# Attention loop of a fused attention and feed-forward kernel: whole loads, row-tiled scores, an earlier decay table, and projections put behind the loop

## The chip, the cores and the metric

The program runs on one core of a Trainium2 chip. Times are microseconds (us) of device time for one launch. Three runs before the change gave a median of 637.87 us (lowest 637.09); the third, 2779.6 us, was a disturbed run and is not used below. Five engines run their own instruction streams in order: PE (matrix products into the 8 banks of PSUM), ACT (activations), DVE (vector), POOL (GpSimd) and SP, which here only starts transfers.

## The reference

Three blocks follow each other. The first is causal linear attention with decay over 2 batches, 8 heads, 768 positions and 64 features, in blocks of 64:

```python
intra = np.einsum('bhic,bhjc->bhij', qb, kb) * Dmask[None]
intra = np.einsum('bhij,bhjd->bhid', intra, vb)
inter = np.einsum('bhid,bhde->bhie', qb * lam_pow[None], kv_state)
out[:, :, sl] = intra + inter
kv_state = lam_block[None, :, None, None] * kv_state + np.einsum('bhsd,bhse->bhde', kb_dec, vb)
```

`Dmask` holds powers of a head's `lam` below the diagonal. The result, 1536 tokens of 512 features, goes through `g(x @ w_in) @ w_out` (2048 hidden features, `g` a clipped square) and then through `(sigmoid(x @ w_gate) * (x @ w_val)) @ w_out` (1536 hidden features).

## The kernel before

**Attention.** The work is cut into 16 units (batch, pair of heads, half of the sequence), each with three chunks of 128 positions. Units 0 to 7 are batch 0. A unit has four products on PE: scores (L412), state updates (L427), and the outputs, from weighted scores (L475) and from states (L484). DVE multiplies the scores by the decay table `DT` (`pT`, L442) and runs the states forward (`sc`, L453), ACT copies states into block-diagonal tiles (`st`, L465), and the output leaves as two float parts, `xh` by ACT (L494) and `xl` by DVE (L495). POOL makes the decayed keys `kd` (L388) and the decayed queries `qs` (L398). `kd` and `pT` need `DT`, `qs` and `sc` need `qp`. Loop i (`for i in range(nu)`) issues scores, updates and `pT` of unit i + 1, `kd` of unit i + 2, outputs of unit i, and `qs` of unit i + 2.

**Tables.** For heads 0 and 1 DVE builds `DT` in 14 steps (L349) and ACT builds `qp` (L354, L357). For the other heads ACT builds rows of powers in `pw` (L360, L363), which go out to DRAM (`pd`, L365) and come back spread over the partitions as `qp` (L370) and `DT` (L375). All these transfers are on SP's queue, among the loads of the units.

**Feed-forward.** A product of float32 accuracy is made of three products of high and low parts. A step of the first block for a slice n of 128 hidden features and a third t of the tokens is `hidden` (12 products, L147 to L149), its activation (L173 to L175), the split into `gh` and `gl` (L165, L166) and `project` (12 products, L202); there are 48 such steps, and 36 of the second block with 24 and 12 products, 2448 products in all. `steps` is a generator that gives such steps one by one. While `rounds` is empty, that is in the attention loop, each `next(steps)` gives either one `hidden` or one `project`. t = 0 needs units 0 to 7 only; t = 1 needs unit 14. Before, the calls stand in loops 7 to 12, 14 and 15.

**Weights.** They come as 68 pieces of 128 x 512 doubles and are turned into two float32 parts in rounds (`w_round`), one piece per stage: ACT takes both words (L85, L86), DVE shifts and joins (L92, L93), `eng` adds (L95), ACT rounds to the high part (L99), `eng` subtracts for the low part (L103). In the attention loop rounds stand in loops 1, 3 and 5 to 12 with POOL as `eng`; behind it DVE does them.

**Order.** `manual_schedule` keeps the written order for each engine, but for a few instructions at the seam between the two blocks of it. Loads and tables wait in SP's stream in order. `wp` is a ring of 14 slots for weight pieces; in its first two lie `q_diag`, copies of the queries of units 0 and 1 with zeros beside each head, so that their scores use 128 rows.

Of the kernel before, what the change touches and what calls it, by code (L numbers as in the profile page):

```python
# [7 lines left out]
F32 = mybir.dt.float32  # L8
# [19 lines left out]
CST = 4 + PADW + P  # L28
FFREE = (13,)
NQD = 2  # L30
NWP, NRAW = 14, 5


@with_exitstack
def fused_kernel(ctx: ExitStack, tc: tile.TileContext, qkv, qd, cst, w1, w2, out):
# [70 lines left out]

    def w_round(eng=dve, between=None):
        k = prog["round"]
        if k - 2 >= len(pieces):
            return  # L110
        if k - 2 >= NWP and pieces[k - 2 - NWP][0] >= prog["done"]:
            return
        prog["round"] += 1
        if 0 <= k - 1 < len(pieces):
            w_float(k - 1, eng)
        if between:
            between()
# [113 lines left out]
    def feed_forward(rounds):  # L231
# [17 lines left out]
        for u in seq:  # L249
# [26 lines left out]
    with ExitStack() as actx:  # L276
# [17 lines left out]
        def u_part(i, o, n):  # L294
            b, p, h = units[i]
            sp.dma_start(out=raw_u[i][:, o:o + n], in_=qkv[b, p, h][:, o:o + n])

        q_diag = {}  # L300

# [3 lines left out]
        DT = kp.tile([P, H, P], F32, name="DT")  # L305
        qp = kp.tile([P, NP, P], F32, name="qp")
        pw = tp.tile([P, 512], F32, tag="c", name="pw")[0:H, 0:2 * P]
        pd = dp.tile([H, 2 * P], F32, name="pd")
# [3 lines left out]
        st = [kp.tile([P, 2 * CU - 1, P], F32, name=f"st{j}") for j in range(2)]  # L312

        def tables():

            cs = tp.tile([P, 512], F32, tag="r", bufs=3, name="cs")
            dm = [tp.tile([P, 512], F32, tag="r", bufs=3, name=f"dm{j}")[:, 0:2 * (PADW + P)]
                  .rearrange("p (h x) -> p h x", h=2) for j in range(2)]
            sp.dma_start(out=cs[:, 0:CST], in_=cst)
            for i in range(NQD):  # L320
                u_load(i)
                q_diag[i] = wp.tile([P, 2, 512], F32, tag="w", name=f"qd{i}").rearrange(
                    "p a b -> p (a b)")[:, 0:2 * UT].rearrange("p (c e t) -> p c e t", c=CU, e=2)
                u_part(i, 1, 1)
                for c in range(CU):
                    if c < 2 or i:
                        c1 = CU if c or i else 1
                        sp.dma_start(out=q_diag[i][:, c:c1], in_=qd[i][:, c:c1])
                    if i:
                        break  # L330
            for i in range(NQD):
                u_part(i, 2, 2)
            for i in range(NQD):
                u_part(i, 0, 1)
            for j in range(2):
# [5 lines left out]
            act.activation(st[1], st[0], AF.Copy)  # L341
            sq = [cs[:, 0:2]] + [cs[:, CST + 2 * k:CST + 2 * k + 2] for k in range(6)]
            for k in range(7):
                w = 1 << k
                if k:
                    pool.tensor_tensor(out=sq[k], in0=sq[k - 1], in1=sq[k - 1], op=ALU.mult)
                for h in range(2):
                    src = cs[:, 4:CST] if k == 0 else dm[k % 2][:, h]
# [4 lines left out]
                    )  # L353
            act.activation(qp[:, 0, 0:1], cs[:, 3:4], AF.Copy)  # L354
            for k in range(7):
                w = 1 << k
                act.activation(qp[:, 0, w:2 * w], qp[:, 0, 0:w], AF.Copy,  # L357
                               scale=qp[:, 0, w - 1:w])

            act.activation(pw[:, P:P + 1], cs[0:H, 2:3], AF.Copy)  # L360
            for k in range(7):
                w = 1 << k
                act.activation(pw[:, P + w:P + 2 * w], pw[:, P:P + w], AF.Copy,  # L363
                               scale=pw[:, P + w - 1:P + w])
            sp.dma_start(out=pd, in_=pw)  # L365
            u_load(2)
            w_load()
            pdv = pd[:, :]
            for e in range(2):
# [4 lines left out]
                )  # L374
            sp.dma_start(  # L375
                out=DT[:, 2:],
                in_=bass.AP(pdv.tensor, pdv.offset + 4 * P, [[1, P], [2 * P, H - 2], [1, P]]),
            )
            u_load(3)
            w_load()  # L380

        S_ps, U_ps, pT, qs, kd, xs = {}, {}, {}, {}, {}, {}

        def pre_k(i):
# [3 lines left out]
            pool.tensor_tensor(  # L388
                out=kd[i], in0=raw_u[i][:, 2].rearrange("p (c h d) -> p c h d", c=CU, h=2),
                in1=DT[:, 2 * p:2 * p + 2, P - 1:P].unsqueeze(1).to_broadcast([P, CU, 2, D]),  # L390
# [3 lines left out]
        def pre_q(i):  # L394
# [3 lines left out]
            pool.tensor_tensor(  # L398
                out=qs[i], in0=raw_u[i][:, 0].rearrange("p (c t) -> p c t", c=CU),
                in1=qp[:, p:p + 1, :].to_broadcast([P, CU, P]), op=ALU.mult,  # L400
            )

        def scores(i):
# [5 lines left out]
            for c in range(CU):  # L409
                for e in range(2):  # L410
                    r = slice(0, P) if i in q_diag else slice(e * D, (e + 1) * D)
                    pe.matmul(  # L412
                        S_ps[i][e][:, c * P:(c + 1) * P], lhsT=u[r, 1, c * P:(c + 1) * P],
                        rhs=q_diag[i][:, c, e] if i in q_diag else u[r, 0, c * P:(c + 1) * P],
                        start=True, stop=True,
                    )

        def updates(i):
# [3 lines left out]
            for c in range(CU):  # L422
                if h * CU + c == 2 * CU - 1:
                    continue
                for e in range(2):
                    r = slice(e * D, (e + 1) * D)
                    pe.matmul(  # L427
                        t[r, c * D:(c + 1) * D], lhsT=kd[i][:, c, e],
                        rhs=u[:, 3, c * P + e * D:c * P + (e + 1) * D],
                        start=True, stop=True,  # L430
# [36 lines left out]
        def outputs(i):  # L467
# [4 lines left out]
            for c in range(CU):  # L472
                for e in range(2):
                    r = slice(e * D, (e + 1) * D)
                    pe.matmul(  # L475
                        x[r, c * P:(c + 1) * P],
                        lhsT=u[:, 3, c * P + e * D:c * P + (e + 1) * D],
                        rhs=pT[i][:, e, c * P:(c + 1) * P],
# [20 lines left out]

        with tc.manual_schedule():  # L500
            tables()
            scores(0)
            scores(1)
# [8 lines left out]
            for i in range(nu):  # L512
# [92 lines left out]
```

## Time and profile before

| what | value |
|---|---|
| median of the runs shown | 637.87 us |
| the profiled execution's own time | 638.09 us |
| its span, first to last instruction | 636.3 us |
| mean granted clock of PE | 0.983 |
| PE busy | 614.8 us, 97% |
| DVE, ACT, POOL busy | 352.5, 287.2, 56.8 us |
| loads and stores | 53.37 MB |

PE is the busiest engine over the span, but the span has stages: up to 96.5 us attention products are mixed with feed-forward products, behind it PE runs feed-forward products without a gap. A busy share over the whole span says nothing of the first stage. The profiled execution took 1.8 us more than its span.

### The profile page before, as it was taken

How to read it: one execution, taken by the hardware profiler on the slowest of the kernel's cores; microseconds unless marked ns; L12 is line 12 of the kernel's file. 1: busy time of each engine (PE TensorE's matmuls, PEld its weight loads, DVE VectorE, ACT ScalarE, POOL GpSimd, SP SyncE). 2: the span in 40 equal slices, each digit the busy share in tenths (PEclk: the TensorE clock that was granted, in tenths of full speed). 3: DMA queues.
4: the chain of work that ended last, by engine and by line, in shares of the span. 5: the costliest groups of instructions: out<-in, count | busy, mean ns of one | idle time of the engine just before them, and what ended most of it. 6: DMA issues, size and time to landing. Idle time of an engine off the chain costs nothing.

```text
span 636.3 us, 7871 instructions
## 1 busy us (share of the span) xinstructions
PE 614.8 (97%) x3072; PEld 507.7 (80%) x3072; DVE 352.5 (55%) x612; ACT 287.2 (45%) x511; POOL 56.8 (9%) x62
## 2 busy tenths in 40 slices
PE   6779889999999999999999999999999999999997
PEld 5667668888888888888888888888888888888886
DVE  4485864655666666666776912157843167713132
ACT  5356745665565556556675612144721145311110
POOL 3486740000000000000000000000000000000000
PEclk9789979999999999999999999999999999999999
DMA  8985520322132223122213400024420022001011
GB/s 262 349 291 220 199 66 1 101 66 67 66 100 66 67 67 91 56 60 92 66 34 99 133 0 1 1 66 133 132 67 0 1 59 74 1 1 67 0 67 66
DMA packets 16229, 53.37 MB, mean 84 GB/s; under 512 B 1720, under 2 KB 3648, under 8 KB 16192
## 3 DMA queue, kind: packets, MB, share of 16 engines
q1 hardware_dynamic: 16192, 52.87, 25.5%
q8 instruction: 24, 0.39, 0.3%
q14 instruction: 13, 0.11, 0.0%
HBM read 49.71 MB, written 3.15 MB: 83 GB/s over the span
## 4 chain that ended last, share of the span: by engine, by line
PE 88%; ACT 4%; DVE 4%; DMA 2%; issue 1%; POOL 1%; SPq 0%; POOLq 0%; ACTq 0%; DVEq 0%
PE a L202 35%; PE h L147 17%; PE h L148 17%; PE h L149 17%; DVE pT L442 1%; DMA DT<-pd 1%; PE x L484 1%; PE x L475 1%; ACT xh L494 1%; ACT st L465 1%; PE s L412 1%; DVE sc L453 1%; DMA pd<-pw 1%; DVE r L175 0%; DVE part L216 0%
## 5 line engine op out<-in xcount | busy, mean ns | idle before, releaser
L147 PE MATMUL h<-xh,w 128*128 128x512 f32 x480 | 188.3, 392 | 0.0
L148 PE MATMUL h<-xh,w 128*128 128x512 f32 x480 | 187.7, 391 | 0.0
L149 PE MATMUL h<-xl,w 128*128 128x512 f32 x480 | 187.3, 390 | 0.0
L202 PE MATMUL a<-gh,w 128*128 128x512 f32 x384 | 118.7, 390 | 0.5 <-DVE r L175 0.5
L148 PEld LDWEIGHTS h<-xh,w 128*128 128x128 f32 x480 | 90.7, 189 | 19.0 <-POOL w L103 0.3
L149 PEld LDWEIGHTS h<-xl,w 128*128 128x128 f32 x480 | 90.6, 189 | 18.9
L147 PEld LDWEIGHTS h<-xh,w 128*128 128x128 f32 x480 | 90.7, 189 | 18.6
L181 DVE TENSOR_TENSOR r<-r,h 128x512 f32<-128x512 f32 x36 | 24.7, 687 | 139.4 <-PE h L149 137.1
L202 PE MATMUL a<-w,gh 128*128 128x512 f32 x288 | 88.6, 389 | 0.0
L202 PEld LDWEIGHTS a<-gh,w 128*128 128x128 f32 x384 | 71.8, 188 | 15.5 <-DVE r L175 0.9
L175 DVE SCALAR_TENSOR_TENSOR r<-r,h 128x512 f32<-128x512 f32 x48 | 33.0, 687 | 87.1 <-ACT r L174 87.0
L165 ACT ACTIVATE gh<-r 128x512 fp32r<-128x512 f32 x84 | 52.4, 624 | 60.8 <-DVE r L181 55.5
L202 PE MATMUL a<-gl,w 128*128 128x512 f32 x192 | 74.7, 389 | 0.0
L173 ACT ACTIVATE r<-h,half 128x512 f32<-128x512 f32 x48 | 33.0, 688 | 91.5 <-PE h L149 91.5
L166 DVE TENSOR_TENSOR gl<-r,gh 128x512 fp32r<-128x512 f32 x84 | 58.4, 695 | 16.5 <-ACT gh L165 16.4
L202 PEld LDWEIGHTS a<-w,gh 128*128 128x128 f32 x288 | 54.1, 188 | 11.2
L180 ACT ACTIVATE r<-h 128x512 f32<-128x512 f32 x36 | 21.5, 597 | 87.2 <-PE h L149 87.2
L99 ACT ACTIVATE w<-wr 128x512 fp32r<-128x512 f32 x68 | 42.4, 623 | 39.6 <-DVE wr L95 39.2
L202 PE MATMUL a<-w,gl 128*128 128x512 f32 x144 | 56.0, 389 | 0.0
L93 DVE SCALAR_TENSOR_TENSOR wr<-raw,wr 128x512 uint32<-128x512 uint32 x68 | 50.1, 737 | 2.3
L85 ACT ACTIVATE wr<-raw 128x512 f32<-128x512 f32 x68 | 45.1, 664 | 0.8 <-POOL w L103 0.8
L86 ACT ACTIVATE wc<-raw 128x512 int32<-128x512 uint32 x68 | 44.8, 658 | 0.0
(51 smaller groups left out, 513.5 us busy)
## 6 DMA issues: line engine op xcount, KB each, us to landing
raw<-in_w SPq DMA_DIRECT2D x68, 512.0 KB, 3.6
u<-in_qkv SPq DMA_DIRECT2D x14, 768.0 KB, 5.7
out<-part SPq DMA_DIRECT2D x12, 256.0 KB, 2.1
u<-in_qkv SPq DMA_DIRECT2D x4, 192.0 KB, 5.6
u<-in_qkv SPq DMA_DIRECT2D x2, 384.0 KB, 6.2
qd<-in_qd SPq DMA_DIRECT2D x1, 384.0 KB, 5.4
DT<-pd SPq DMA_DIRECT2D x1, 384.0 KB, 6.3
qd<-in_qd SPq DMA_DIRECT2D x1, 256.0 KB, 3.7
```

Source lines behind the costliest of these rows:

```text
L85: act.activation(r, hi.bitcast(F32), AF.Copy, scale=2.0 ** -112)
L86: act.activation(c, lo, AF.Copy, scale=2.0 ** -29)
L93: dve.scalar_tensor_tensor(out=ru, in0=hi, scalar=0x80000000, in1=ru, op0=ALU.bitwise_and, op1=ALU.bitwise_or)
L99: act.activation(ws[i][:, 0], tmps[i][1], AF.Copy)
L147: pe.matmul(h, lhsT=wh, rhs=xh[:, k, tt], start=(k == 0), stop=False)
L148: pe.matmul(h, lhsT=wl, rhs=xh[:, k, tt], start=False, stop=False)
L149: pe.matmul(h, lhsT=wh, rhs=xl[:, k, tt], start=False, stop=(k == NP - 1))
L165: act.activation(gh, g, AF.Copy)
L166: dve.tensor_tensor(out=gl, in0=g, in1=gh.bitcast(F32), op=ALU.subtract)
L173: act.activation(r, h, AF.Relu, bias=half, scale=0.5)
L175: dve.scalar_tensor_tensor(out=r, in0=r, scalar=1.0, in1=h, op0=ALU.min, op1=ALU.max)
L202: pe.matmul(accs[j], lhsT=a, rhs=b_, start=(f == 0 and m == 0), stop=(f == GF - 1 and m == 2))
```

## The change

It does these things:

- The first four units load into two slots each of `wp`, as halves (q and k, then k and v by rows), with whole slices; units 0 to 2 are loaded ahead of all tables. Loads of later units are asked for two loops earlier (`u_load(i + 6)`), into the same four buffers.
- `q_diag` and its input are no longer used: scores of units 0 and 1 use 64 rows like the others.
- `warm` gives PE two products of zeros ahead of the first scores.
- ACT's queue loads the constants and stores `pd`; ACT builds `pw` ahead of `qp`; `DT` comes back in two transfers, heads 2 and 3 first. DVE builds its two tables one head after the other.
- Rounds stand in loops 3 to 6 and 8 to 14. Up to loop 6 DVE subtracts for the low part, later POOL.
- `next(steps)` stands in loops 7, 9, 11 and 13, and gives one `hidden` each; no `project` is given in the loop. Behind it the generator first catches up with two of them.

```diff
-FFREE = (13,)
+HIDDEN = (7, 9, 11, 13)
+ROUNDS = (3, 4, 5, 6, 8, 9, 10, 11, 12, 13, 14)
 NQD = 2
+NEARLY = 4
+WARM = 2
...
-    def w_round(eng=dve, between=None):
+    def w_round(eng=dve, between=None, low=dve):
...
         if 0 <= k - 2:
-            w_low(k - 2, eng)
+            w_low(k - 2, low)
...
-            flushed = False
-            if len(behind) == LAG:
+            while len(behind) >= (LAG if rounds else LAG + 1):
                 flushed = finish()
-                if not rounds:
-                    yield u
-            if rounds:
                 if ph:
...
-            raw_u[i] = up.tile([P, 4, UT], F32, tag="u", name=f"u{i}")
-            if i >= NQD:
-                sp.dma_start(out=raw_u[i], in_=qkv[b, p, h])
...
+            if i < NEARLY:
+
+                t = [wp.tile([P, 2, 512], F32, tag="w", name=f"u{i}_{j}")
+                     .rearrange("p a b -> p (a b)")[:, 0:2 * UT]
+                     .rearrange("p (a t) -> p a t", a=2) for j in range(2)]
+                for j in range(2):
+                    sp.dma_start(out=t[j], in_=qkv[b, p, h][:, 2 * j:2 * j + 2])
+            else:
+                a = up.tile([P, 4, UT], F32, tag="u", name=f"u{i}")
+                sp.dma_start(out=a, in_=qkv[b, p, h])
...
+        def warm():
+
+            z = bank("z")
+            for _ in range(WARM):
+                pe.matmul(z, lhsT=zero[:, 0:P], rhs=zero, start=True, stop=True)
...
-            sp.dma_start(out=cs[:, 0:CST], in_=cst)
-            for i in range(NQD):
+            act.dma_start(out=cs[:, 0:CST], in_=cst)
+            for i in range(3):
                 u_load(i)
...
-            sp.dma_start(out=pd, in_=pw)
-            u_load(2)
-            w_load()
...
+            act.dma_start(out=pd, in_=pw)
...
-            sp.dma_start(
-                out=DT[:, 2:],
-                in_=bass.AP(pdv.tensor, pdv.offset + 4 * P, [[1, P], [2 * P, H - 2], [1, P]]),
-            )
+            for h0, h1 in ((2, 4), (4, H)):
+                sp.dma_start(
+                    out=DT[:, h0:h1],
+                    in_=bass.AP(pdv.tensor, pdv.offset + h0 * 2 * P,
+                                [[1, P], [2 * P, h1 - h0], [1, P]]),
+                )
             u_load(3)
+            u_load(4)
+            w_load()
+            u_load(5)
             w_load()
...
-                    r = slice(0, P) if i in q_diag else slice(e * D, (e + 1) * D)
+                    r = slice(e * D, (e + 1) * D)
...
             tables()
+            warm()
             scores(0)
...
-                if i in (1, 3) or 5 <= i <= 12:
-                    w_round(pool, finish)
+                if i in ROUNDS:
+                    w_round(pool, finish, pool if i >= nu // 2 else dve)
...
-                u_load(i + 4)
+                u_load(i + 6)
                 w_load()
-                if i >= nu // 2 - 1 and i not in FFREE:
+                if i in HIDDEN:
                     next(steps)
```

The first place is ACT's stream at the start. Before:

```order
L341 ACT_TABLE_LOAD
L341 ACTIVATE st_98<-st_97 128x640
L354 ACTIVATE qp<-cs 128x1
L357 ACTIVATE qp<-qp 128x1
...
L360 ACTIVATE pw<-cs 8x1
L363 ACTIVATE pw<-pw 8x1
...
L363 ACTIVATE pw<-pw 8x64
```

And with the change:

```order
L326 DMA cs<-in_cst 128x196
L336 ACT_TABLE_LOAD
L336 ACTIVATE st_99<-st_98 128x640
L338 ACTIVATE pw<-cs 8x1
L341 ACTIVATE pw<-pw 8x1
...
L341 ACTIVATE pw<-pw 8x64
L343 DMA pd<-pw 8x256
L344 ACTIVATE qp<-cs 128x1
```

The eight steps of `pw` stand ahead of those of `qp`, and the store follows them on the same engine. The second place is SP's stream from the store on, before:

```order
L365 DMA pd<-pw 8x256
L292 DMA u_162<-in_qkv 128x1536
L78 DMA raw_164<-in_w 128x512
L370 DMA qp<-pd 64x3x128 x2
L375 DMA DT<-pd 128x6x128
L292 DMA u_169<-in_qkv 128x1536
```

And with the change, from the last of the six early loads on:

```order
L295 DMA u_1_115<-in_qkv 128x768
L363 DMA qp<-pd 64x3x128
L363 DMA qp<-pd 64x3x128
L369 DMA DT<-pd 128x2x128
L369 DMA DT<-pd 128x4x128
L295 DMA u_0_167<-in_qkv 128x768
L295 DMA u_1_168<-in_qkv 128x768
L298 DMA u_171<-in_qkv 128x1536
L81 DMA raw_173<-in_w 128x512
```

Unit 2 now stands ahead of the tables, the first weight piece behind units 3 and 4. The third place is PE's stream at the last unit, before (`x` are outputs, `h` a `hidden`, `a` a `project`):

```order
L475 MATMUL x_987<-pT_943,u_775 64x128 x6
L484 MATMUL x_987<-qs_912,st_98 128x128 x2
L147 MATMUL h_1_0_998<-xh,w_454 128x512
...
L475 MATMUL x_1019<-pT_980,u_844 64x128 x6
L484 MATMUL x_1019<-qs_965,st_98 128x128 x3
L202 MATMUL a_0_0_0_779<-gh_0_861,w_835 128x512 x2
```

And with the change:

```order
L473 MATMUL x_967<-pT_887,u_628 64x128 x6
L482 MATMUL x_967<-qs_868,st_99 128x128 x2
L473 MATMUL x_987<-pT_957,u_681 64x128
L205 MATMUL a_0_0_0_1011<-gh_0_698,w_619 128x512 x2
L205 MATMUL a_0_0_0_1011<-gl_0_699,w_619 128x512
L473 MATMUL x_987<-pT_957,u_681 64x128 x5
L482 MATMUL x_987<-qs_919,st_99 128x128 x3
```

No `hidden` stands between the outputs of the last two units any more, and the first `project` of all begins inside the last unit.

## Rows read from the trace of the kernel before

**Rows 1.** The page: busy us of each engine, its share, instructions.
```profile
PE 614.8 (97%) x3072; PEld 507.7 (80%) x3072; DVE 352.5 (55%) x612; ACT 287.2 (45%) x511; POOL 56.8 (9%) x62
```
**Rows 2.** Windows by stage: length; each engine's busy us (instructions); clock, DMA share, GB/s.
```profile
0.00:20.10 20.10, 10.78 (x74) 9.12 (x74) 8.30 (x28) 8.39 (x23) 6.67 (x19) 0.94 0.88 284
20.10:42.70 22.60, 18.57 (x234) 15.64 (x234) 15.95 (x39) 12.86 (x28) 15.15 (x16) 0.88 0.92 327
42.70:87.80 45.10, 40.95 (x350) 32.46 (x350) 31.98 (x61) 27.21 (x54) 34.94 (x29) 0.92 0.55 198
96.50:632.00 535.50, 535.50 (x2364) 443.47 (x2363) 291.76 (x477) 235.60 (x401) 0.00 (x0) 1.00 0.18 57
```
**Rows 3.** The chain that ended last, first 21 us: start, length, what.
```profile
2.03 0.74 ACT st L341
...
5.28 0.10 ACT pw L360
...
7.84 3.47 DMA pd<-pw
...
12.71 6.33 DMA DT<-pd
...
19.20 0.84 POOL kd L388
```
**Rows 4.** Transfers issued in the first 60 us: count, size, median us to landing.
```profile
cs<-in_cst SPq DMA_DIRECT2D x1, 98.0 KB, 1.9
```
**Rows 5.** Timeline of PE: first scores, then state updates of units 2 to 9, 15.
```profile
4.46 1.19 PE L412 MATMUL s<-qd,u 128*128 128x128 f32 x4 [4.46 <-DMA qd<-in_qd]
...
20.09 0.91 PE L427 MATMUL uu<-u,kd 128*64 128x64 f32 x12 [3.99 <-POOL kd L388]
...
25.03 0.45 PE L427 MATMUL uu<-u,kd 128*64 128x64 f32 x8
...
27.58 0.57 PE L427 MATMUL uu<-u,kd 128*64 128x64 f32 x12
...
30.47 0.45 PE L427 MATMUL uu<-u,kd 128*64 128x64 f32 x8
...
34.17 0.57 PE L427 MATMUL uu<-u,kd 128*64 128x64 f32 x12 [1.09 <-POOL kd L388]
...
37.06 0.45 PE L427 MATMUL uu<-u,kd 128*64 128x64 f32 x8
...
42.71 0.91 PE L427 MATMUL uu<-u,kd 128*64 128x64 f32 x12 [2.20 <-POOL kd L388]
...
51.04 0.45 PE L427 MATMUL uu<-u,kd 128*64 128x64 f32 x8
...
87.77 0.69 PE L427 MATMUL uu<-u,kd 128*64 128x64 f32 x8
```
**Rows 6.** Timeline of POOL: the low-part subtraction of two rounds that follow each other.
```profile
43.85 1.27 POOL L103 TENSOR_TENSOR w<-wr,w 128x512 fp32r<-128x512 f32 x1
...
48.71 1.30 POOL L103 TENSOR_TENSOR w<-wr,w 128x512 fp32r<-128x512 f32 x1
```
**Rows 7.** Timeline of DVE: the first weighting of units 7 and 8, round between.
```profile
34.90 0.55 DVE L442 TENSOR_TENSOR pT<-s,DT 128x384 f32<-128x384 f32 x1
...
38.41 0.55 DVE L442 TENSOR_TENSOR pT<-s,DT 128x384 f32<-128x384 f32 x1
```
**Rows 8.** The chain again, 42 to 51 us: feed-forward products at both clocks.
```profile
46.48 0.43 PE h L147
...
49.09 0.23 PE h L148
```
**Rows 9.** Waits from 42 to 97 us: total us, times, longest.
```profile
PE s L412 <- DVE pT L442: 2.1, 2, 1.1
```
**Rows 10.** Timeline of PE at the end of attention: a `hidden` starts; last outputs.
```profile
90.85 0.77 PE L147 MATMUL h<-xh,w 128*128 128x512 f32 x1
...
95.54 0.94 PE L484 MATMUL x<-qs,st 128*128 128x128 f32 x6
```

More of the change, by code (lines that the diff above doesn't have):

```diff
@@ L289, in u_load @@
             b, p, h = units[i]
-            raw_u[i] = up.tile([P, 4, UT], F32, tag="u", name=f"u{i}")
-            if i >= NQD:
-                sp.dma_start(out=raw_u[i], in_=qkv[b, p, h])
[L294 to L300, printed above, removed]
+            if i < NEARLY:
[7 more added lines that the diff above has]
+                sp.dma_start(out=a, in_=qkv[b, p, h])
+                t = [a[:, 0:2], a[:, 2:4]]
+            raw_u[i] = [t[j // 2][:, j % 2] for j in range(4)]
         DT = kp.tile([P, H, P], F32, name="DT")
         qp = kp.tile([P, NP, P], F32, name="qp")
+        zero = tp.tile([P, 512], F32, tag="c", name="zero")
         pw = tp.tile([P, 512], F32, tag="c", name="pw")[0:H, 0:2 * P]
@@ L318, in tables @@
                   .rearrange("p (h x) -> p h x", h=2) for j in range(2)]
-            sp.dma_start(out=cs[:, 0:CST], in_=cst)
-            for i in range(NQD):
+            act.dma_start(out=cs[:, 0:CST], in_=cst)
+            for i in range(3):
                 u_load(i)
[L322 to L334, printed above, removed]
+            dve.memset(zero, 0.0)
             for j in range(2):
@@ L341, in tables @@
             act.activation(st[1], st[0], AF.Copy)
-            sq = [cs[:, 0:2]] + [cs[:, CST + 2 * k:CST + 2 * k + 2] for k in range(6)]
+            act.activation(pw[:, P:P + 1], cs[0:H, 2:3], AF.Copy)
             for k in range(7):
                 w = 1 << k
-                if k:
-                    pool.tensor_tensor(out=sq[k], in0=sq[k - 1], in1=sq[k - 1], op=ALU.mult)
-                for h in range(2):
+                act.activation(pw[:, P + w:P + 2 * w], pw[:, P:P + w], AF.Copy,
+                               scale=pw[:, P + w - 1:P + w])
+            act.dma_start(out=pd, in_=pw)
+            act.activation(qp[:, 0, 0:1], cs[:, 3:4], AF.Copy)
+            for k in range(7):
+                w = 1 << k
+                act.activation(qp[:, 0, w:2 * w], qp[:, 0, 0:w], AF.Copy,
+                               scale=qp[:, 0, w - 1:w])
+            sq = [cs[:, 0:2]] + [cs[:, CST + 2 * k:CST + 2 * k + 2] for k in range(6)]
+            for k in range(1, 7):
+                pool.tensor_tensor(out=sq[k], in0=sq[k - 1], in1=sq[k - 1], op=ALU.mult)
+            for h in range(2):
+                for k in range(7):
+                    w = 1 << k
                     src = cs[:, 4:CST] if k == 0 else dm[k % 2][:, h]
@@ L353, in tables @@
                     )
[L354 to L364, printed above, removed]
-            sp.dma_start(out=pd, in_=pw)
-            u_load(2)
-            w_load()
             pdv = pd[:, :]
@@ L388, in pre_k @@
             pool.tensor_tensor(
-                out=kd[i], in0=raw_u[i][:, 2].rearrange("p (c h d) -> p c h d", c=CU, h=2),
+                out=kd[i], in0=raw_u[i][2].rearrange("p (c h d) -> p c h d", c=CU, h=2),
                 in1=DT[:, 2 * p:2 * p + 2, P - 1:P].unsqueeze(1).to_broadcast([P, CU, 2, D]),
@@ L398, in pre_q @@
             pool.tensor_tensor(
-                out=qs[i], in0=raw_u[i][:, 0].rearrange("p (c t) -> p c t", c=CU),
+                out=qs[i], in0=raw_u[i][0].rearrange("p (c t) -> p c t", c=CU),
                 in1=qp[:, p:p + 1, :].to_broadcast([P, CU, P]), op=ALU.mult,
@@ L410, in scores @@
                 for e in range(2):
-                    r = slice(0, P) if i in q_diag else slice(e * D, (e + 1) * D)
+                    r = slice(e * D, (e + 1) * D)
                     pe.matmul(
-                        S_ps[i][e][:, c * P:(c + 1) * P], lhsT=u[r, 1, c * P:(c + 1) * P],
-                        rhs=q_diag[i][:, c, e] if i in q_diag else u[r, 0, c * P:(c + 1) * P],
+                        S_ps[i][e][:, c * P:(c + 1) * P], lhsT=u[1][r, c * P:(c + 1) * P],
+                        rhs=u[0][r, c * P:(c + 1) * P],
                         start=True, stop=True,
@@ L428, in updates @@
                         t[r, c * D:(c + 1) * D], lhsT=kd[i][:, c, e],
-                        rhs=u[:, 3, c * P + e * D:c * P + (e + 1) * D],
+                        rhs=u[3][:, c * P + e * D:c * P + (e + 1) * D],
                         start=True, stop=True,
@@ L476, in outputs @@
                         x[r, c * P:(c + 1) * P],
-                        lhsT=u[:, 3, c * P + e * D:c * P + (e + 1) * D],
+                        lhsT=u[3][:, c * P + e * D:c * P + (e + 1) * D],
                         rhs=pT[i][:, e, c * P:(c + 1) * P],
```

## The prediction

> **What bounds the kernel now.** The page comes first: PE is busy 97% of the span [rows 1]. That figure mixes stages, so the windows come next [rows 2]. From 96.5 us on PE is busy all of 535.50 us with 2364 products, 0.2265 us each, at the full clock; DVE and ACT have time to spare there (291.76 and 235.60 us). Nothing in that stage can be shortened except by having fewer products left when it begins. Of the 2448 feed-forward products, 84 lie ahead of it (five `hidden`, two `project`). So the time is: end of the attention loop, plus 0.2265 us for each product still to do, plus a tail of about 4 us, plus the 1.8 us between span and time.
>
> The stage before 96.5 us has several limits. At the start the chain of waits [rows 3] is one line: ACT builds the powers (from 5.28 us on), the store `pd` takes 3.47 us, the copy back into `DT` 6.33 us, and POOL's `kd` of unit 2 starts at 19.20. PE starts unit 2's updates at 20.09 after an idle time of 3.99 [rows 5]. I call that moment U(2), and likewise for the other units; U(i + 1) lies in loop i. From 20.1 to 42.7 the transfer engines are busy 92% at 327 GB/s [rows 2]. From 42.7 to 87.8 no engine is full (PE 40.95 of 45.10 us, POOL 34.94): there in-order engines wait for each other in turn.
>
> **The change, part by part.** *Projections out of the loop.* 48 products instead of 84 are done in it, so 36 x 0.2265 = 8.15 us of PE work go behind it, where nothing hides them. That is the price; the loop has to end 8.15 us earlier to pay it.
>
> *The table.* ACT's eight `qp` steps run from the end of L341 (2.77) to 5.28 [rows 3]; moved behind `pw`, they give 2.5 us back, of which the new issue on ACT's queue takes about 0.4 (an estimate from SP's pace of the same issue). The store leaves at 7.84 - 2.1 = 5.7 us. It took 3.47 us on SP's queue behind loads [rows 3]; a transfer with nothing ahead took 1.9 [rows 4]. I take the middle, 2.7, since loads are still in flight: landed at 8.4. From landing to the issue of `DT` are 1.4 us (11.31 to 12.71), so 9.8. The first copy now has a third of the bytes; it lands after at least 1.9 and at most 6.33 us; I take 3.8, because the large load that was queued ahead of it (unit 2, and a weight piece) is now either done or behind it, while the small pieces stay small. `kd` and PE's start add 0.9: U(2) at 14.5 instead of 20.09, a gain of 5.6. Ends: 12.6 and 17.8.
>
> The Trainium skill, "DMA: Bandwidth & Descriptors", section on queues, rings and completion order, says that a transfer engine takes turns between queue rows packet by packet, so that ACT's store need not stand behind SP's loads. By it the store would take the 1.9 us of rows 4 and the sum would be 0.8 us better; by the row of the store alone it would be 0.8 worse.
>
> *Loops to U(8).* Six intervals took 42.71 - 20.09 = 22.6 us [rows 5]. With the change: 3.7 for the first (unit 3's load is now issued behind the table copies), 2.55 and 2.9 for the next two (the intervals from 25.03 to 27.58 to 30.47), 3.7 for the one with the first joining of words (30.47 to 34.17), and 5.1 each for the last two, whose rounds are whole, 23.1 in all. The 5.1 is a choice between the 2.9 of 34.17 to 37.06 and the 5.6 of 37.06 to 42.71; it is near the upper end because DVE's subtraction now stands in a line L93, POOL, ACT, DVE and holds up the next unit's weighting. Loads give the same: a unit and a piece are 1.31 MB, 4.0 us at 327 GB/s. Loss 0.5; U(8) at 37.6. Ends: 20 and 27 for the six.
>
> *Loops to U(15).* Seven intervals took 87.77 - 42.71 = 45.1 us [rows 5]. The first had a `hidden` at the low clock and took 8.3; the other six took 6.1 on the mean. With the change the first keeps its `hidden` and has no round: 6.0, between 5.6 (12 products and 2.9 us of attention products, the interval from 27.58 that had nothing else on PE) and 8.3. Three have a round and a `hidden`: 6.3, the old mean and a little, because one of the old six had no step. Three have a round alone: POOL repeats a round in 48.71 - 43.85 = 4.86 us when it never rests [rows 6]; DVE came round in 38.41 - 34.90 = 3.5 [rows 7]. I take 4.5, nearer to POOL's, which may spread its work over two loops. Sum 6.0 + 3 x 6.3 + 3 x 4.5 = 38.4, gain 6.7.
>
> *The end.* From U(15) to the end of the last outputs (95.54 + 0.94 = 96.48) were 8.7 us [rows 5, 10], with a `hidden` of t = 1 from 90.85 that now comes later. Half of its 12 products ran at 0.43 and half at 0.23 us [rows 8]; 3.6 us go. This product count is in the 36 above.
>
> *What costs nothing.* Scores on 64 rows and whole slices: PE's first work waits for loads (4.46 us idle [rows 5]) and then for `kd`; the bytes of `q_diag` make room for unit 2, so the first 2.4 MB stay 2.4 MB. Without that cover it would be a microsecond of scores either way. Zero products: four records of 512 columns, four times the 1.19 us of four records of 128 [rows 5], end near 6 us, while the first updates have to wait for DVE's table and POOL's `kd`. If the scores did hold them up, 1.5 us. DVE's table by heads: 14 steps in a chain, at most 1 us later by my estimate, and `kd` of unit 0 needs a load besides. Units in weight slots: six of 14 slots are free for the first pieces, and the others are released long before piece 6. The additional round and the two rounds right behind the loop: some 6 us of DVE, while PE has two `project`, a `hidden`, another `project` and `hidden` queued, 60 x 0.2265 = 13.6 us. If that cover failed, a `gl` would be late and PE would stand for what is missing.
>
> *Sum.* 5.6 - 0.5 + 6.7 + 3.6 = 15.4 us earlier, less 8.15: 7.2. From the profiled 638.09 this gives **630.9**; the median of the runs is 0.2 lower, which I leave out.
>
> **The rivals.** *The clock (slower).* PE's clock fell where PE waited: before U(8), after a wait of 2.20 [rows 5], and before U(15), after two waits of 2.1 together [rows 9]. In a loop with a round alone PE would have 2.9 us of work in 4.5, so such waits may come each time. The price is seen in the interval after U(8): 8.3 against 5.6, 2.7 us. The sum holds at most one fall, as before. With three more it is 630.9 + 8.1 = 639.0, with four 641.7: slower than before from the third on. Against it: at the low clock PE takes longer and so stops waiting, and in loops 3 to 6 with rounds the clock mostly held (0.88 on the mean [rows 2]). Chance 0.13, at **640**.
>
> The Trainium skill, "TensorE: Matmul & The Clock Gate", section on the clock gate, says it plainly: "the default state is throttled, and activity releases the throttle." By that rule filler products are what keeps attention fast, and this change takes 36 away.
>
> *The projections were free (no change).* If the in-order chain of ACT and DVE sets the loops and POOL takes 4.86 anyway, the six intervals stay at 6.1 and the first at 8.3. Then 6.7 goes out of the sum: 637.6. For it speaks that no engine was full there; against it that a loop without a `hidden` spares ACT three and DVE two instructions of the chain. Chance 0.14.
>
> *The table gains little (it does not do what it says).* If store and copies wait among the early loads as before, U(2) comes at 17.8: 634.2. For it: all transfers use the same engines, and they were busy 88% in that stage. Chance 0.16.
>
> *Everything runs at PE's or DVE's pace (faster).* A round alone at 3.5, with a `hidden` 5.6, the first 5.3: 5.3 + 3 x 9.1 = 32.6 instead of 38.4; and loads far ahead, 22 instead of 23.1 for the six. That is 6.9 us more: **624.0**. POOL's 4.86 speaks against it. Chance 0.18.
>
> **How the numbers follow.** My forecast has 0.39, with a range of its own of 627 to 634.5. The range over the cases is 624.0 to 639.0: it leaves out most of the clock's case (0.1) and half of the fast one (0.09). About 2%, 12.8 us, can be told from no change. Faster than 625.3 is most of the fast case and little else, 0.12; slower than 650.9 takes a failure beyond all of these, 0.03; the rest is 0.85.
>
> **What will show it.** U(2) between 13 and 16 us, and the copy of heads 2 and 3 landing ahead of unit 3. U(8) near 37.6. Loops with a round alone at 4 to 5 us, with POOL without rest; if they take 6, the projections were free. The clock from U(8) to U(15): below 0.85 means the clock's case. The last outputs near 81 us, then 2400 products without a gap. A wait of PE behind the loop for `gl` or a weight would make the prediction wrong in a way that no case here holds.

## The result, and the profile after

The changed kernel takes 630.43 us (median; 630.17 to 630.62). The kernel before took 637.01, 637.09 and 637.87 on the same chip; a fourth run of 2779.6 us was disturbed and is left out. The ratio of the mean times is 0.9892 [0.9872, 0.9911] (95% interval), 6.9 us less. The prediction was 630.9. The profiled execution took 630.28 us for a span of 628.3, against 638.09 and 636.3. So 8.0 us of span have to be found.

The page's first part of the changed kernel (engine, busy us, share, instructions) answers to [rows 1]:

```profile
PE 608.9 (97%) x3076; PEld 500.8 (80%) x3076; DVE 356.5 (57%) x613; ACT 287.8 (46%) x511; POOL 57.0 (9%) x62
```

The share has not moved; it could not have told where the time went. The windows of the changed kernel (stretch and length, busy us and instructions of PE, PEld, DVE, ACT and POOL, granted clock, DMA share, GB/s) answer to [rows 2]:

```profile
0.00:14.50 14.50, 9.06 (x60) 5.80 (x60) 8.06 (x26) 7.47 (x20) 5.93 (x17) 0.84 0.61 204
14.50:37.00 22.50, 20.40 (x250) 17.04 (x250) 16.57 (x41) 11.22 (x26) 14.55 (x15) 0.88 0.96 381
37.00:80.00 43.00, 34.87 (x368) 27.42 (x365) 36.23 (x68) 29.15 (x59) 33.79 (x29) 1.00 0.60 214
...
90.00:624.00 534.00, 534.00 (x2358) 442.17 (x2357) 287.11 (x468) 232.28 (x395) 0.00 (x0) 1.00 0.18 55
```

The last row: behind 90 us PE has no gap, at 534.00 / 2358 = 0.2265 us a product, as before. The third: from 37 to 80 us the clock is full in this execution (0.92 before, from 42.7 to 87.8), though PE is busy only 34.87 of 43 us; in a second profile of the same kernel it was 0.96 (experiment 12). The second: loads run at 381 GB/s where they ran at 327.

PE's timeline of the changed kernel (start, us, engine, line, operation, count, idle time before it and what ended it) answers to [rows 5, 10]:

```profile
11.56 1.49 PE L425 MATMUL uu<-u,kd 128*64 128x64 f32 x20 [3.98 <-POOL kd L386]
17.07 0.57 PE L425 MATMUL uu<-u,kd 128*64 128x64 f32 x12
19.96 0.45 PE L425 MATMUL uu<-u,kd 128*64 128x64 f32 x8
22.51 0.57 PE L425 MATMUL uu<-u,kd 128*64 128x64 f32 x12
25.40 0.45 PE L425 MATMUL uu<-u,kd 128*64 128x64 f32 x8
28.50 0.57 PE L425 MATMUL uu<-u,kd 128*64 128x64 f32 x12
33.17 0.45 PE L425 MATMUL uu<-u,kd 128*64 128x64 f32 x8 [1.49 <-POOL kd L386]
37.35 0.57 PE L425 MATMUL uu<-u,kd 128*64 128x64 f32 x12
...
43.19 0.50 PE L150 MATMUL h<-xh,w 128*128 128x512 f32 x1 [1.66 <-ACT xh L492]
...
45.09 0.45 PE L425 MATMUL uu<-u,kd 128*64 128x64 f32 x8
47.63 0.57 PE L425 MATMUL uu<-u,kd 128*64 128x64 f32 x12
53.92 0.45 PE L425 MATMUL uu<-u,kd 128*64 128x64 f32 x8 [0.56 <-POOL kd L386]
58.59 0.57 PE L425 MATMUL uu<-u,kd 128*64 128x64 f32 x12 [2.04 <-POOL kd L386]
64.70 0.45 PE L425 MATMUL uu<-u,kd 128*64 128x64 f32 x8 [0.42 <-POOL kd L386]
69.56 0.57 PE L425 MATMUL uu<-u,kd 128*64 128x64 f32 x12 [2.24 <-POOL kd L386]
75.23 0.45 PE L425 MATMUL uu<-u,kd 128*64 128x64 f32 x8
...
78.18 0.43 PE L473 MATMUL x<-pT,u 128*64 128x128 f32 x2 [1.20 <-DVE pT L440]
...
80.23 0.94 PE L482 MATMUL x<-qs,st 128*128 128x128 f32 x6
```

These are U(2) = 17.07, U(8) = 37.35, U(9) = 45.09 and U(15) = 75.23; the last outputs end at 80.23 + 0.94 = 81.17, 15.3 us earlier than the 96.48 of before. Of the 36 moved products three now run before that point, so 33 x 0.2265 = 7.5 us of them come behind it. 15.3 - 7.5 = 7.8: the 8.0 us are found, within 0.2.

### The profile page after: what moved, and what is told of

It reads as the page before. It is cut to its first block, busy times and chain, and to the rows that moved or that the text cites. A ratio compares the mean times of both kernels' runs of the same rounds, so it can differ in the third digit from the quotient of the medians.

```text
span 628.3 us, 7878 instructions
## 1 busy us (share of the span) xinstructions
PE 608.9 (97%) x3076; PEld 500.8 (80%) x3076; DVE 356.5 (57%) x613; ACT 287.8 (46%) x511; POOL 57.0 (9%) x62
## 4 chain that ended last, share of the span: by engine, by line
PE 88%; DVE 6%; ACT 3%; issue 2%; DMA 1%; POOL 0%; ACTq 0%; POOLq 0%
PE a L205 36%; PE h L150 17%; PE h L152 17%; PE h L151 17%; DVE pT L440 2%; DVE sc L451 1%; ACT st L463 1%; ACT xh L492 1%; DMA cs<-in_cst 1%; DVE wr L96 0%; PE x L473 0%; DVE w L106 0%; DVE part L219 0%; DVE xl L493 0%; ACT w L102 0%
## 5 line engine op out<-in xcount | busy, mean ns | idle before, releaser
L169 DVE TENSOR_TENSOR gl<-r,gh 128x512 fp32r<-128x512 f32 x84 | 59.1, 704 | 16.6 <-ACT gh L168 16.6
L96 DVE SCALAR_TENSOR_TENSOR wr<-raw,wr 128x512 uint32<-128x512 uint32 x68 | 51.2, 753 | 2.3
L88 ACT ACTIVATE wr<-raw 128x512 f32<-128x512 f32 x68 | 45.1, 663 | 0.2 <-POOL w L106 0.2
```

What stands on the lines that cost most here:

```text
L88: act.activation(r, hi.bitcast(F32), AF.Copy, scale=2.0 ** -112)
L96: dve.scalar_tensor_tensor(out=ru, in0=hi, scalar=0x80000000, in1=ru, op0=ALU.bitwise_and, op1=ALU.bitwise_or)
L169: dve.tensor_tensor(out=gl, in0=g, in1=gh.bitcast(F32), op=ALU.subtract)
```

## The experiments

Each kernel is compared with the kernel before on the chip it ran on: the two medians, then the ratio of the mean times with its 95% interval. Unless said otherwise an edit is made to the changed kernel.

**1. The projections stay in the loop**, with the old generator; everything else is as in the change.

```diff
-            while len(behind) >= (LAG if rounds else LAG + 1):
+            flushed = False
+            if len(behind) == LAG:
                 flushed = finish()
+                if not rounds:
+                    yield u
+            if rounds:
...
-                if i in HIDDEN:
+                if i >= nu // 2 - 1 and i not in (13,):
```

> The changed kernel, but with the generator and the step places of before: hidden in loops 7 to 9, 11 and 14, project in 10, 12 and 15. Theory A (the forecast): moving the projections behind the loop shortened it by a little more than their 8.15 us, 6.7 + 3.6 against 8.15, so this kernel takes 2.1 us more than the changed one, about 632.5. Rival (they were free filler in the loop): the loop is no longer than in the changed kernel and 36 products are done in it for nothing, 630.4 - 8.15 = 622.3. Rival (they cost much more than their products, since each lengthens the chain of ACT and DVE): 635 or more.

Measured: 639.80 against 636.56, 1.0045 [1.0031, 1.0059], about 3 us slower where the change is 6.9 us faster. It can't be read as the price of the projections, since the later rounds came into it. PE's timeline of this kernel:

```profile
56.33 0.60 PE L150 MATMUL h<-xh,w 128*128 128x512 f32 x1 [4.21 <-ACT w L102]
...
58.10 0.80 PE L151 MATMUL h<-xh,w 128*128 128x512 f32 x1 [1.18 <-POOL w L106]
```

The `hidden` of a loop waited 4.21 us for the weight that the same loop's round was making, and the granted clock from 37 to 80 us was 0.85. Here a late round did harm because a `hidden` needed its weight at once. The next two runs take the parts again, each with rounds that fit.

**2. Only the projections moved** (in the kernel before, its own rounds and start).

```diff
-            flushed = False
-            if len(behind) == LAG:
+            while len(behind) >= (LAG if rounds else LAG + 1):
                 flushed = finish()
-                if not rounds:
-                    yield u
-            if rounds:
...
-                if i >= nu // 2 - 1 and i not in FFREE:
+                if i in (7, 9, 11, 13):
```

> The kernel before with one thing changed: generator and step places as in the changed kernel (hidden in loops 7, 9, 11, 13, no project in the loop); table, loads, rounds as before. Theory A: 2.1 us less than before, 635.4. Free filler: 8.15 us more at most, up to 645. If they cost much more than their products: 633 or less. If start and steps are independent, this and proj_in_loop add up to the whole change, 7.05 us.

Measured: 641.12 against 636.56, 1.0062 [1.0043, 1.0082]: slower. PE's timeline at the last unit:

```profile
81.30 0.45 PE L423 MATMUL uu<-u,kd 128*64 128x64 f32 x8 [0.43 <-POOL kd L384]
86.45 0.69 PE L471 MATMUL x<-pT,u 128*64 128x128 f32 x2 [3.40 <-DVE pT L438]
```

U(15) came at 81.30, 6.5 us earlier than before, so the loops did shrink. Then unit 15's weighting stood on DVE behind the steps of two rounds, PE waited 3.40 us, and the clock was low behind it; the last outputs ended at 91.8, 10.5 us after U(15), where the change needs 5.9. The earlier end did not pay the 8.15 us.

**3. Only the loop** (in the kernel before: experiment 2 and the change's rounds, with the low subtraction where the change has it).

```diff
-                if i in (1, 3) or 5 <= i <= 12:
-                    w_round(pool, finish)
+                if i in (3, 4, 5, 6, 8, 9, 10, 11, 12, 13, 14):
+                    w_round(pool, finish, pool if i >= nu // 2 else dve)
```

> The kernel before with its own start and loads, but the loop of the change: hidden in loops 7, 9, 11, 13, no project, rounds in loops 3 to 6 and 8 to 14, low part on DVE up to loop 6. In only_proj_moved the rounds ended with loop 12, and two rounds of DVE came to stand ahead of the weighting of unit 15, for which PE waited 3.4 us; here they stand behind. Theory: U(8) to the last outputs takes 44 us instead of 54, less 8.15: 634.5 to 635.5. Rival (the loss of only_proj_moved was the projections themselves, not the place of the rounds): 640 or more.

Measured: 634.46 against 637.14, 0.9963 [0.995, 0.9976]: 2.7 us less. U(15) at 79.37, last outputs at 85.3, 5.9 us later. Between experiments 2 and 3 lie only the places of the rounds, one more of them inside the loop, and the engine of the low subtraction in loops 5 and 6; together these make 6 us (by the ratios) to 7 us (by the medians, 4.6 + 2.7).

**4. Only the start** (experiment 1 with ten rounds as before, the one of loop 1 in loop 4, and the low subtraction on POOL: the loop of before behind the new start).

```diff
-ROUNDS = (3, 4, 5, 6, 8, 9, 10, 11, 12, 13, 14)
+ROUNDS = tuple(range(3, 13))
...
-                    w_round(pool, finish, pool if i >= nu // 2 else dve)
+                    w_round(pool, finish, pool)
```

> The changed kernel with its start and loads, but the loop of before: generator and step places of before, rounds in loops 3 to 12 with POOL throughout, so that from loop 5 on each round stands where it did and no hidden meets a weight of its own loop (as it did in proj_in_loop, where PE waited 4.2 us for the high part). Theory (parts add up): the start brings U(8) forward by some 5 us as in the changed kernel, and loops and end are those of before: 631.5 to 633. Rival (the loop or the seam takes it back, by waits or by the clock): 635 or more.

Measured: 633.24 against 637.14, 0.9943 [0.9925, 0.996]: 3.9 us less, U(2) at 16.48. The two parts give 3.9 + 2.7 = 6.6, the change 6.9: they add, within intervals of about a microsecond each. The start is taken as a whole here; what its parts (slots, earlier loads, scores on 64 rows, order of the tables) are worth singly was not tried.

**5. The constants back on SP's queue**, ahead of the loads.

```diff
-            act.dma_start(out=cs[:, 0:CST], in_=cst)
+            sp.dma_start(out=cs[:, 0:CST], in_=cst)
```

> The changed kernel with the load of the constants as SP's first transfer again, as before; the store of the table stays on ACT's queue. Theory: on ACT's queue the constants shared the transfer engines with the big loads and took 4.11 us instead of 1.9, which delays DVE's and ACT's tables by 2.2 us and with them units 0 to 2; if nothing else is close behind, 628.2 and U(2) near 15. Rival (the loads of units 2 to 6 are the limit, POOL's kd waits for them at 18.1, 24.4 and 27.6 us): the start is earlier but U(6) is not, 630.4.

Measured: 632.21 against 636.56, 0.9925 [0.9911, 0.9939]: not better than the change, and U(2) at 17.61. My theory fell. DVE and ACT did begin 2.1 us earlier and the store left at 5.35 instead of 7.49, but the copies that wait for it could be issued only at 10.77, later than the 9.77 of the change.

**6. Constants on SP, unit 2 behind the tables, DVE's heads in turns.**

```diff
-            act.dma_start(out=cs[:, 0:CST], in_=cst)
-            for i in range(3):
+            sp.dma_start(out=cs[:, 0:CST], in_=cst)
+            for i in range(2):
...
-            for h in range(2):
-                for k in range(7):
+            for k in range(7):
+                for h in range(2):
...
+            u_load(2)
```

> The changed kernel with three edits of its start: constants as SP's first transfer, DVE's two tables built in turn as before, unit 2 loaded behind the table copies. In cst_on_sp the store left 2.1 us earlier and landed 1.0 us later than in the changed kernel: it seems to land when the loads in flight have drained, on whichever queue. Theory (so it is the loads ahead of it that hold it): with two units instead of three in flight it lands by 8.5 us, U(2) comes at 15 or earlier and the loads of units 3 to 6 follow sooner: 627.5 to 629. Rival (unit 2 is then late instead): 630 to 631.

Measured: 632.36 against 637.14, 0.9929 [0.991, 0.9948]. Now the store left at 5.4 and the copies were issued at 8.06, but unit 2 landed at 15.5 (PE's scores of it waited 4.29 us), and U(2) was 17.40, U(3) 22.42 against 19.96. Three orders of the early transfers give U(2) between 17.07 and 17.61.

Windows of one us show when the early loads end: for each kernel the last with such loads and the one behind it. The changed kernel's:

```profile
8.00:9.00 1.00, 0.00 (x0) 0.00 (x0) 0.93 (x4) 0.84 (x4) 0.00 (x0) 1.00 0.65 259
9.00:10.00 1.00, 0.00 (x0) 0.00 (x0) 0.89 (x4) 0.90 (x4) 0.00 (x0) 0.89 0.00 1
```

The windows of experiment 5:

```profile
9.00:10.00 1.00, 0.57 (x12) 0.43 (x12) 0.00 (x0) 0.00 (x0) 1.00 (x2) 1.00 0.49 195
10.00:11.00 1.00, 0.78 (x12) 0.72 (x14) 0.93 (x4) 0.00 (x0) 1.00 (x2) 0.75 0.04 14
```

The windows of experiment 6:

```profile
6.00:7.00 1.00, 0.12 (x4) 0.06 (x2) 1.00 (x4) 0.87 (x4) 0.26 (x1) 1.00 0.79 316
7.00:8.00 1.00, 1.00 (x18) 0.88 (x20) 0.13 (x1) 0.90 (x4) 0.68 (x2) 1.00 0.04 14
```

In the last column (GB/s) the loads end between 8 and 9, at about 10 and at about 7 us, and the copies, which wait for the store, were issued at 9.77, 10.77 and 8.06: about a microsecond later each time. When the store left (7.49, 5.35, 5.4) does not order these times; when the loads ended does. This is read from three kernels.

**7. Without the zero products.**

```diff
-WARM = 2
+WARM = 0
```

> The changed kernel without the two products of zeros. Theory: they do not touch a wait, and the clock falls in the start anyway (9.6 to 16.4 us in the changed kernel): 630.4, no change. Rival (they shift the times at which the clock rises and falls, so that units 0 to 8 run more at the low clock without them): 631.5 to 633.

Measured: 630.12 against 637.14, 0.9892 [0.9874, 0.991]: the change's own ratio, so in the total they cost and bring nothing that can be told. But my theory's reason was wrong: the clock did not fall in the start. A window of this kernel, with the granted clock third from the end, and PE's timeline at U(2):

```profile
0.00:37.00 37.00, 24.80 (x308) 20.52 (x308) 25.54 (x66) 19.11 (x47) 20.70 (x32) 1.00 0.86 321
```

```profile
15.95 0.57 PE L425 MATMUL uu<-u,kd 128*64 128x64 f32 x12
```

The changed kernel has 0.86 there. U(2) came at 15.95, 1.1 us earlier than with the zero products, right behind POOL's `kd` of unit 2 (14.98 + 0.84). Of that 0.4 us was left at U(8) (36.98 for 37.35), where PE waited for `kd` again. Over the span the five runs without zeros had a mean clock of 0.996 to 0.997, the eight runs of the changed kernel 0.985 to 0.995.

**8. The low subtraction on POOL in every loop**, as before.

```diff
-                    w_round(pool, finish, pool if i >= nu // 2 else dve)
+                    w_round(pool, finish, pool)
```

> The changed kernel with the low-part subtraction on POOL in loops 5 and 6 too. Theory: on DVE it stood in the chain twice, 1.5 us each, ahead of the weighting; on POOL it hides, 627.5 to 629. Rival (POOL then makes the kd of units 8 and 9 late, as in the kernel before where PE waited 2.2 us for it ahead of U(8)): 630 to 632.

Measured: 630.01 against 636.56, 0.9896 [0.9876, 0.9916]: no difference. U(8) came at 38.91 after a wait of 2.96 for POOL's `kd`, and the loop behind it took 7.2 instead of 7.7.

**9. The subtraction on DVE in loops that have a round alone.**

```diff
-                    w_round(pool, finish, pool if i >= nu // 2 else dve)
+                    w_round(pool, finish, pool if i in HIDDEN else dve)
```

> The changed kernel with the low-part subtraction on DVE in every round that stands without a hidden in its loop (3 to 6, 8, 10, 12, 14), and on POOL in loops 9, 11, 13. Theory (POOL sets the pace of the late loops: PE waits 2.04 and 2.24 us for its kd at 58.6 and 69.6): these waits go, two to three pairs of loops each lose about 1 us, ratio to before 0.984 to 0.986, that is 2 to 3 us less than the changed kernel. Rival (DVE's subtraction then stands ahead of the next weighting, 1.5 us under contention, as in loops 5 and 6): ratio 0.989 to 0.992.

Measured: 635.32 against 637.32, 0.9967 [0.9953, 0.9981]: 4.9 us worse than the change on the same chip (630.47), where I had expected a gain. POOL was relieved, as meant. The window from 37 to 80 us of this kernel, with POOL's busy time fifth:

```profile
37.00:80.00 43.00, 36.30 (x348) 28.91 (x348) 30.98 (x64) 27.93 (x56) 28.82 (x26) 0.92 0.58 207
```

PE's timeline of this kernel up to the last unit:

```profile
69.78 0.57 PE L425 MATMUL uu<-u,kd 128*64 128x64 f32 x12 [2.90 <-POOL kd L386]
...
81.27 0.69 PE L473 MATMUL x<-pT,u 128*64 128x128 f32 x2 [2.21 <-DVE pT L440]
```

POOL's busy time fell from 33.79 to 28.82, and PE still waited 2.90 for `kd`: in that window POOL stood 14.2 us ahead of its additions to the words (L98). The profile puts most of these waits down to ACT's `xh`, but L98 doesn't read it: it adds to what DVE joins at L96, and it began about 0.15 us after L96's end each time. So POOL was late for what DVE gave it, not for its load. The seam cost more (2.21 for `pT`, clock 0.83 from 80 to 90 us). Which of these makes the 4.9 us I have only read from this trace, not tried apart.

**10. The `hidden` products and one round a loop later.**

```diff
-HIDDEN = (7, 9, 11, 13)
-ROUNDS = (3, 4, 5, 6, 8, 9, 10, 11, 12, 13, 14)
+HIDDEN = (8, 10, 12, 14)
+ROUNDS = (3, 4, 5, 7, 8, 9, 10, 11, 12, 13, 14)
```

> The changed kernel with hidden in loops 8, 10, 12, 14 and the round of loop 6 moved to loop 7. Theory (the loop after U(8) took 7.7 us because the first hidden waits for the high part of unit 7, which ACT makes behind a state copy that waits for DVE): one loop later that part is long ready, PE's 1.66 us of waiting go, ratio 0.986 to 0.987. Rival (the last step now lies in loop 14 and makes the end longer by its 2.7 us): ratio 0.989 to 0.992.

Measured: 628.73 (628.45 to 629.04) against 637.32, 0.9864 [0.9849, 0.988]: the best of all, 1.7 us below the change on the same chip. PE's timeline of this kernel:

```profile
36.95 0.57 PE L425 MATMUL uu<-u,kd 128*64 128x64 f32 x12 [1.56 <-POOL kd L386]
39.84 0.45 PE L425 MATMUL uu<-u,kd 128*64 128x64 f32 x8
45.14 0.57 PE L425 MATMUL uu<-u,kd 128*64 128x64 f32 x12
...
77.67 0.94 PE L482 MATMUL x<-qs,st 128*128 128x128 f32 x6
```

The loop behind U(8) takes 2.9 us instead of 7.7, and the next one, which has the first `hidden` now, 5.3 instead of 2.5: together 8.2 instead of 10.3. The last outputs end at 78.6 instead of 81.2, and the three `project` products that ran ahead of that point now come behind it (0.7 us). From U(10) to the last outputs both kernels take 33.5 us, so but for 0.4 us ahead of U(8) the gain lies in these two intervals.

**11. Experiments 9 and 10 together.** The two edits as above.

> Both edits together: hidden in 8, 10, 12, 14, round of loop 6 in loop 7, low part on DVE where a round has no hidden. If the gains add: ratio 0.981 to 0.983. If they take from each other: that of the better one.

Measured: 629.92 against 637.32, 0.9887 [0.9868, 0.9906]. No better than the change, 1.2 us worse than experiment 10 alone: the subtraction on DVE loses here too, if less.

**12. The change once more**, unedited, beside experiments 9 to 11.

> The changed kernel itself, to be compared with the other three on one chip: ratio 0.989 by its first runs.

Measured: 630.47 against 637.32, 0.9891 [0.9875, 0.9908]. The time repeats, but the profile does not in all. PE's timeline of this second execution at U(14) and U(15):

```profile
69.82 0.57 PE L425 MATMUL uu<-u,kd 128*64 128x64 f32 x12 [2.23 <-POOL kd L386]
...
70.98 1.63 PE L482 MATMUL x<-qs,st 128*128 128x128 f32 x6
...
77.06 0.45 PE L425 MATMUL uu<-u,kd 128*64 128x64 f32 x8
```

Behind the wait of 2.23 the clock fell this time: the six outputs from states took 1.63 us instead of 0.94, the granted clock was at its lower level from 71.0 to 74.5 us, and U(14) to U(15) took 7.2 instead of 5.7. In return it had not fallen ahead of U(8), where the first execution had it low from 33.7 to 37.1. The span was 629.0 for 628.3.

## Why the prediction was right, point by point

The total was 0.5 us off, and the last outputs came at 81.17 where "near 81" stood. That is better than the steps deserve: three of the five were wrong by more than 2 us, and that the errors cancelled was luck.

| step | predicted | measured | off | second profile (experiment 12) |
|---|---|---|---|---|
| U(2) | 14.5 | 17.07 | 2.6 late | 16.82 |
| six loops to U(8) | 23.1 | 20.3 | 2.8 early | 20.8 |
| U(8) to U(9) | 6.0 | 7.7 | 1.7 late | 7.7 |
| U(9) to U(15) | 32.4 | 30.1 | 2.3 early | 31.7 |
| U(15) to the last outputs' end | 5.1 | 5.9 | 0.8 late | 4.8 |

Of the signs named beforehand two did not come: U(2) between 13 and 16 us, and POOL without rest (it was busy 33.79 of 43 us). Of the three loops with a round alone two took 4 to 5 us. The copy of heads 2 and 3 ahead of unit 3, U(8), the clock above 0.85, the last outputs and PE without a gap behind them came as named.

**The table: right in sign, wrong in its main term.** The chain of the changed kernel that ended last, at its start (start, us, what), answers to [rows 3, 4]:

```profile
0.74 4.11 DMA cs<-in_cst
...
10.66 0.85 POOL kd L386
```

DVE's timeline there, the first and the last step of the table:

```profile
4.87 0.38 DVE L356 SCALAR_TENSOR_TENSOR dm<-cs 128x128 f32<-128x128 f32 x1 [3.18 <-DMA cs<-in_cst]
...
10.23 0.35 DVE L356 SCALAR_TENSOR_TENSOR DT<-dm,cs 128x128 f32<-128x128 f32 x1
```

SP's timeline, the issues of the copies:

```profile
9.77 1.32 SPq L363 DMA_DIRECT2D qp<-pd  x2
11.13 1.12 SPq L369 DMA_DIRECT2D DT<-pd  x2
```

POOL's timeline, `kd` of unit 2:

```profile
15.19 0.84 POOL L386 TENSOR_TENSOR kd<-u,DT 128x384 f32<-128x384 f32 x1 [0.98 <-DMA DT<-pd]
```

The page's list of DMA issues, the first copy (KB, us to landing):

```profile
DT<-pd SPq DMA_DIRECT2D x1, 128.0 KB, 3.8
```

I had given the moved constants 0.4 us on ACT's queue and no later landing. On that queue, beside six loads, they took 4.11 us instead of the 1.9 of [rows 4], so ACT and DVE began about 2.2 us later and the store left at 7.49, not 5.7. It landed after 2.3 us (2.7 predicted), the copies were issued at 11.13 (9.8), the first took 3.8 (3.8): `kd` of unit 2 began at 15.19. The other 1.0 us is PE's: it waited 3.98 for `kd` of unit 0, was at the low clock from 9.8 to 16.6 us, and came to unit 2 only at 17.07. That wait has a cause that I had priced at 1 us at most: DVE builds the table head after head from 4.87 to 10.58, 5.7 us, where the same 14 steps in turns had taken 2.69 to 6.53, 3.8 us. And the low clock goes with the zero products, which I had put under what costs nothing: without them (experiment 7) PE waited 3.20 for the same `kd`, the clock stayed full, and U(2) came at 15.95.

But the mis-sized term could not be had back by undoing it: experiment 5 lands the constants early and the store late. The Trainium skill, "DMA: Bandwidth & Descriptors", section on queues, rings and completion order, has two rules that bear on it. From the turns between queue rows I had worked out 1.9 us for the store: 2.3, 5.4 and 2.6 us after it left the copies could go, so the traces do not agree with that estimate; whether the rows took turns can't be read from them. The same section says that the completion signal is a strongly ordered write that "lands only after every earlier write from that SDMA engine, across its queues". The six window rows above agree with that one; as a cause it is inferred, since no run moved the store alone.

**The six loops** needed 20.3 us, near the lower end of 20. Loads ran at 381 GB/s instead of the 327 on which I had put 4.0 us a unit, and the first of the six took 2.9, not 3.7. The two with whole rounds took 4.67 and 4.18 for my 5.1. The start alone (experiment 4) gives 3.9 us of time, with 22.1 us for these six loops and the old rounds.

**The loop behind U(8)** was the second miss. I had given it a `hidden` and no round. The chain of the changed kernel, 38 to 44 us, shows what I left out:

```profile
38.16 0.64 ACT w L102
...
38.83 1.46 DVE w L106
...
42.65 0.50 ACT xh L492
...
43.19 0.50 PE h L150
```

The round of loop 6 ends inside it: ACT's `w` and DVE's low subtraction stand ahead of unit 8's weighting and states. ACT makes `xh` of unit 7 behind its copies of those states, so it is late, and PE waits 1.66 us for it in the middle of its `hidden` (1.69 in the second profile). Experiment 10 takes `hidden` and round out of these loops, and the wait goes. It moves both at once; which of them does it stays open.

**The other six.** With a `hidden` 6.3, 6.1 and 5.7 for my 6.3; with a round alone 2.5, 4.7 and 4.9 for my 4.5. POOL did set the pace there, with waits of 2.04 and 2.24 for `kd`, in two of the three. The first was free, since POOL began that round only after U(10) = 47.63. POOL's timeline:

```profile
48.92 1.29 POOL L98 TENSOR_TENSOR wr<-wr,wc 128x512 int32<-128x512 int32 x1 [5.21 <-ACT xh L492]
```

The profile names ACT's `xh`, which ended at 48.89; but L98 reads what DVE joins at L96, and L96 ended at 48.77. In this kernel L98 began 0.14 to 0.18 us after L96's end whenever POOL had stood before it, so POOL had stood for DVE.

**The seam.** It came near its price, 5.9 and 4.8 for 5.1. The 3.6 us for the `hidden` were too few by my own rows: 6 x 0.43 + 6 x 0.23 = 3.96, which makes 4.7. And I had not seen that the seam could go wrong. Experiment 2 shows the case: the same products moved, two rounds ahead of the last weighting, 10.5 us, and the kernel slower than before. This is what the new places of the rounds are worth.

**The rivals.** *The clock* did not come in the profiled execution: 1.00 from 37 to 80 us, two falls in all (9.8 to 16.6 and 33.7 to 37.1) where there were three. But the kernel is not safe from it. The second fall stood behind a wait of 1.49, while the waits of 2.04 and 2.24 brought none; in experiment 12 the same wait of 2.23 did, and so did one of 2.05 in experiment 7 and one of 2.23 in experiment 2. How long PE waits once does not tell it alone. Longer waits did go with falls (4.21 in experiment 1, 3.40 in experiment 2). The Trainium skill, "TensorE: Matmul & The Clock Gate", section on the clock gate, says that activity releases the throttle; the prediction drew from it that filler products keep attention fast. The traces do not bear that conclusion out: with 36 products fewer in the loop PE's mean granted clock over the span was 0.991 in both profiles, 0.983 before. *The projections were free* is refuted by the loops: from U(8) to U(15) 37.9 us for 45.1, and 38.9 in experiment 2, where only the projections moved. *The table gains little* was near: U(2) at 17.07 lies nearer to its 17.8 than to my 14.5. *Everything at PE's or DVE's pace* held from U(2) to U(6) only, 2.5 to 3.1 us each. Of what was to cost nothing, the two rounds behind the loop did: PE never waited for `gl` or a weight there. The zero products cost about a microsecond at U(2) and nothing that can be told in the total (experiment 7).

## What to carry to other kernels

Work that fills PE in an attention loop can be moved behind it at a gain, but only if the steps that ride on the loop are placed again: the same move was 4.6 us slower with the old places, 2.7 us faster with new ones, and one loop later again gave 1.7 us. To bring a small store forward, look at which loads are in flight when it leaves, since here those who waited for it could go about a microsecond after the loads had ended, whenever it had left. And when a forecast comes true, add up its steps before trusting them: here 2.6 + 1.7 + 0.8 us late stood against 2.8 + 2.3 early. A second profile of the same kernel belongs to that: it showed which of these steps repeat.

## What the runs showed of the hardware that was not expected

- A transfer of 98 KB on ACT's queue took 4.11 us beside six loads of SP's queue, 1.9 in SP's first place. The 8 KB store took 2.3 to 5.4 us until those who wait for it could go, and that moment followed the end of the loads by about a microsecond in three kernels.
- The changed kernel, profiled twice, had its second stretch of low clock at two places (33.7 to 37.1 and 71.0 to 74.5 us), behind waits of 1.49 and 2.23 us, at nearly the same time in all (630.28 and 631.06).
- DVE's low subtraction (L106) took 1.46 and 1.50 us in loops 6 and 5, where it began while POOL ran an addition of the same round (L98); the median of its 61 is 0.685. Both ended 0.55 us after that L98 had ended. The Trainium skill, "SBUF — State Buffer", section on SBUF's two separate sides, describes this: a port pair of DVE and POOL that one of them holds for a whole instruction. The trace agrees.
- Fourteen steps of DVE, two chains of seven in which each step needs the one before, took 5.7 us with one chain after the other (changed kernel and experiment 5) and 3.8 us with the two in turns (kernel before and experiment 6).
